# Cosine attention and a gated feed-forward on one core: the third tiles of batches 2 and 4 join pairs that run across two batches

## Chip, cores and metric

One core of a Trainium2 chip. The metric is the device time of one execution in microseconds (us). Three executions of the kernel before gave 402.96, 403.22 and 403.63 us; the median is 403.22 us.

## What is computed

The reference, cut to what matters: attention with normalised queries and keys, then a feed-forward layer with a clipped gate, then the output product.

```python
q_n = q / (norm(q) + 1e-06); k_n = k / (norm(k) + 1e-06)      # q, k, v: 8 x 12 x 448 x 64
attn = softmax(q_n @ k_n.T / tau)
x = (attn @ v).transpose(0, 2, 1, 3).reshape(3584, 768)
h = x @ w_in                                                   # 768 x 2048
g = h * clip(h + 3, 0, 6) / 6
out = g @ w_out                                                # 2048 x 768
```

The change lies in the last line, the **second product** `g @ w_out`.

## The kernel before

**Stages.** Twelve heads of a batch are worked on two at a time, so a batch has six turns and the kernel 48, numbered 0 to 47. A table of operations (`PLAN`) orders the first 18 turns, a loop over `i` the turns 18 to 47, and a table (`LAST`) what comes after them. While turn `i` does attention for its two heads of batch `i // 6`, TensorE also works off *units* of the feed-forward layer of an earlier batch, taken from `units[i]` in the order that is written there. Nothing is scheduled by itself: each engine works its own instructions in the order in which the code issues them.

**A turn of the loop, on TensorE.** Six score products (line 442) into the six PSUM banks of a ring, the remaining value products of the turn before (line 482), one unit, the seventh score product, the other units, and the first value products of this turn. A unit takes the next bank of the ring and may start only when the last reader of that bank is done.

**Units.** An `F` (`mm1_unit`, line 587) is one of the 16 column blocks of `x @ w_in` of a batch: six matmuls of 128x448, then a relu on ScalarE (line 596) and a product on VectorE (line 602) that writes the block's rows of `g` into the buffer `gT` (two buffers, for even and odd batches). The second product works on tiles of 128 tokens. A batch of 448 tokens has three and a half of them: an even batch keeps three whole tiles (0 to 2), and its last 64 tokens are copied (`g_left`) into the next batch's buffer, where they form tile 3 of the odd batch. Two tiles make a *pair*.

**Seven products for a pair.** With the tiles as rows and the two halves of the 2048 columns as columns, a pair is a 2x2 block matrix. `product_unit` multiplies it by the 2x2 blocks of `w_out` with seven block products instead of eight, named 1 to 7, of eight matmuls of 128x384 each (line 788). The names in the code are `product.pair`: 5.4 is product 5 of pair 4. VectorE makes five sums of blocks of `g` for a pair (`g_sum`, line 766): 7, 6 and 1 into buffers of their own (`gs`), 5 and 2 in place in `gT`. Products 2, 5 and 6 run on into the bank of 4, 3 and 1 after that bank has been read, or, written `2a` and `5a`, into a bank of their own, and are then added on GpSimd (line 829). ScalarE copies 3 and 4 into the buffers `d` and `e` (line 836) and 5 and 2 into output tiles (line 807, or 825 for `2a` and `5a`). GpSimd then makes `e = d + e`, `d = e - 5` and `e = e - 2` (lines 817, 818, 821). VectorE adds product 1 to `d` in place (line 845; product 6 waits for that, since it uses the bank of 1) and writes 6 + `e` and 7 + `d` out (line 813). There are two buffers `d`, used in turn by the pairs, and one `e`.

**Lone tiles.** Of an even batch tiles 0 and 1 are a pair, and tile 2 is left alone. `single_unit` (line 868) multiplies it by two units of 16 matmuls of 128x384, `s2.0` and `s2.1` for batch 2, after one sum (`e`) on VectorE, and VectorE copies each result out (line 878).

**What sets the order.** `TURNS` lists the products of each turn; the code mixes them with that turn's `F` units: two or three `F` and one or two products, the last of them at the turn's end. `side` lists the sums that VectorE makes at the start of a turn, before the turn's units. GpSimd works per turn: in odd turns first two copies of keys (`km`, line 399), then a square (line 236), a normalisation (line 293), a cast of values (line 312), and at the end what the pairs ask for. The queue of SyncE carries loads, stores and the two transposing transfers that bring normalised keys and queries (`tT`, line 350) and attention results (`xT`, lines 528 and 540) into place, all in program order.

Of the kernel before, what the change touches and what calls it, by code (L numbers as in the profile page):

```python
# [59 lines left out]
]  # L60

LAST = [
# [3 lines left out]
]  # L66
H_BY, M1_BY = "vvvvvvpp", "pppvpppp"

# [2 lines left out]
def kernel(  # L71
# [11 lines left out]
    B, H, S, D = q.shape  # L83
# [4 lines left out]
    NP = B * HP  # L88
# [576 lines left out]


    LEFT, RIGHT = slice(0, MH), slice(MH, 2 * MH)
    PAIRS = [p for b in range(0, B, 2) for p in (((b, 0), (b, 1)), ((b + 1, 3), (b + 1, 0)), ((b + 1, 1), (b + 1, 2)))][1:]
    LOOP = 8
    summed, g_summed, issued_products = set(), set(), set()  # L670
    banks, parts, ready = {}, {}, set()
    late_sums = [
# [36 lines left out]
    def sum_of(n, what):  # L709

        if what == "e":
            return gs["1"] if n < B - 2 else late_sums[1]["e"]
        if n < LOOP or n == len(PAIRS) - 1:
            return gs[what + str(n % 2) if what == "7" else what]
        return late_sums[n % 2][what]

    def d_and_e(n):
        if n < LOOP:
# [29 lines left out]
    def g_sum(n, what):  # L748

        if what == "e":  # L750
            t = 2 + n % 2
            o, x, y, op = sum_of(n, "e"), half(n, t, 0), half(n, t, 1), ALU.add
        else:
            a11, a12, a21, a22 = (block(n, i, k) for i in range(2) for k in range(2))
# [11 lines left out]
        nc.vector.tensor_tensor(out=o[:, :, :], in0=x, in1=y, op=op)  # L766
        g_summed.add((n, what))

    def product_unit(n, name, end=None, apart=False):

        need = {"3": ["y3"], "4": ["y4"], "1": "1", "6": "6", "7": "7"}.get(name, [])
        assert all((x, c) in summed for x in need for c in range(KC))
        if name not in "34":
            assert (n, name) in g_summed
        base = None if apart else {"2": "4", "5": "3", "6": "1"}.get(name)
        if base is None:
            banks[n, name] = bank_of(None, 1)
        ps, key = banks.pop((n, base)) if base else banks[n, name]
        c0, width = (MH // 2 * end, MH // 2) if end in (0, 1) else (0, MH)
        if name in "167":  # L780
            lhs, rhs = sum_of(n, name), w_sum[name]
        else:
            i, k = {"3": (0, 0), "4": (1, 1), "2": (1, 0), "5": (0, 1)}[name]
            m = LEFT if name in "42" else RIGHT
            lhs, rhs = block(n, i, k), w_out_sb[:, :, m].rearrange("p (c k) m -> p c k m", k=2)[:, :, k, :]
        m = ps[:, c0 : c0 + width]
        for c in range(KC):
            nc.tensor.matmul(  # L788
                m,
                lhs[:, c, :],  # L790
                rhs[:, c, c0 : c0 + width],
                start=(base is None and c == 0),
                stop=(c == KC - 1),
                skip_group_check=True,
            )
        issued_products.add((n, name))
        d, e = d_and_e(n)
        if base is None and name in "34":
            unread[key] = 1 + ((n, name) not in APART)

        def done(i, o, cols):
            unread[key] = 0
            result(*PAIRS[n][i], cols, o, end)

        def copied(i, cols):
            o = out_tile()
            nc.scalar.copy(out=o[:, :], in_=m)
            parts[n, name] = o
            done(i, o, cols)

        def added(i, cols, x):
            parts[n, name] = o = out_tile()
            nc.vector.tensor_tensor(out=o[:, 0:width], in0=m, in1=x[:, c0 : c0 + width], op=ALU.add)
            done(i, o, slice(cols.start + c0, cols.start + c0 + width))

        def both():
            nc.gpsimd.tensor_tensor(out=e, in0=d, in1=e, op=ALU.add)
            nc.gpsimd.tensor_tensor(out=d, in0=e, in1=parts[n, "5"][:, :], op=ALU.subtract)

        def rest():  # L820
            nc.gpsimd.tensor_tensor(out=e, in0=e, in1=parts[n, "2"][:, :], op=ALU.subtract)

        def added_later(i, cols, x):
            parts[n, name] = o = out_tile()
            nc.scalar.copy(out=o[:, :], in_=m)
            unread[key] = 0

            def add():
                nc.gpsimd.tensor_tensor(out=o[:, :], in0=o[:, :], in1=x, op=ALU.add)
                result(*PAIRS[n][i], cols, o)  # L830

            post["p"].append(add)

        def finish():
            if name in "34":
                nc.scalar.copy(out={"3": d, "4": e}[name], in_=m)
                unread[key] -= 1
            elif apart:
                added_later(*{"5": (0, RIGHT, d), "2": (1, LEFT, e)}[name])
            elif name == "5":  # L840
                copied(0, RIGHT)
            elif name == "2":
                copied(1, LEFT)
            elif name == "1":
                nc.vector.tensor_tensor(out=d, in0=m, in1=d, op=ALU.add)
# [214 lines left out]
    def products(text):  # L1060
# [10 lines left out]

    TURNS = {
# [5 lines left out]
    }  # L1078
    APART = {(n, y) for n in range(len(PAIRS)) for x, y in (("5a", "3"), ("2a", "4")) if f"{x}.{n}" in " ".join(TURNS.values()).split()}
    side = {  # L1080
        18: [(weight_sums, "y4", KC // 2, KC // 2)], 19: sums(0, "62"), 20: sums(0, "1"),
        21: sums(1, "75"), 22: sums(1, "621"),
        25: sums(2, "75"), 26: sums(2, "62"), 27: sums(2, "1"), 28: [(g_left, 2)], 29: sums(2, "e"),
        31: sums(3, "75"), 32: sums(3, "62"), 33: sums(3, "1"),
        34: sums(4, "75"), 35: sums(4, "621"), 37: [(g_left, 4)],
        38: sums(5, "75"), 39: sums(5, "62"), 40: sums(5, "1"), 41: sums(4, "e"),
        43: sums(6, "75"), 44: sums(6, "62"), 45: sums(6, "1"), 46: sums(7, "75"), 47: sums(7, "62"),
    }
    w_sums = [(w_sum_of, x, p) for p in range(FCN // 4) for x in "15672"]
    late = {44: "p", 45: "ppppp", 46: "pp"}  # L1090
# [2 lines left out]
    for b in range(2, B - 1):  # L1093
        first = firsts(b, *range(FCN))
        for n, x in enumerate([0, 3, 3, 3, 3, 2]):
            i = (b + 1) * HP + n
            u = carry + [first.pop(0) for _ in range(x)]
            carry = []
            *p, last = products(TURNS[i])
# [7 lines left out]

    assert len(carry) == 2
    units[NP] = [x for line in LAST for x in listed(line)]
    units[NP] += products("3.9 4.9") + sums(9, "1") + products("5.9") + sums(10, "75") + products("2.9 3.10") + sums(10, "62")  # L1110
    units[NP] += products("4.10 5.10") + sums(10, "1") + products("2.10 1.9 1.10")
    units[NP] += [(product_unit, n, x, 2) for n, x in ((9, "7"), (9, "6"), (10, "6"))]
    units[NP] += [(product_unit, 10, "7", x) for x in range(2)]

    FG = d_ff // 4
    weights = [
# [198 lines left out]
```

## Time and profile before

| | |
|---|---|
| median of 3 executions | 403.22 us |
| profiled execution, its own time | 403.54 us |
| its span, first to last instruction | 401.7 us |
| outside the span (403.54 - 401.7) | 1.8 us |
| mean granted TensorE clock | 0.998 |
| TensorE matmul busy | 392.0 us, 98% |
| VectorE, ScalarE, GpSimd busy | 300.9, 280.2, 262.8 us |

How to read it: a group row gives line, engine, operation, the tiles written and read, the shape and a count, then busy time and the mean length of one in ns. A row of the timeline gives the start and length of an instruction, or of a run of like ones (x8), and in brackets how long its engine had been idle before it and for whom it waited. Matmuls overlap, so a run of eight ends later than the next one starts; the distance between starts is what a unit costs.

### The profile page before, as it was taken

The numbers are of one execution on the slowest core, as the hardware profiler recorded it, in microseconds if no ns is written. First come the engines' busy times: TensorE is split into PE (matmuls) and PEld (weight loads), VectorE is DVE, ScalarE is ACT, GpSimd is POOL, SyncE is SP. The second block draws the span as 40 slices with busy tenths as digits, with TensorE's granted clock in tenths as the row PEclk, the third lists the DMA queues.
The fourth block names the chain that finished last, engine by engine and source line by source line (L and its number), as shares of the span: only waits on it lengthen the run. The fifth ranks groups of instructions, "written<-read, shape, count | busy, mean of one in ns | idle before, by whom it ended". The sixth has DMA issues, their size and how long they took to land.

```text
span 401.7 us, 9814 instructions
## 1 busy us (share of the span) xinstructions
PE 392.0 (98%) x3743; PEld 239.4 (60%) x3743; DVE 300.9 (75%) x535; ACT 280.2 (70%) x615; POOL 262.8 (65%) x253
## 2 busy tenths in 40 slices
PE   7988999999999999999999999999999999999996
PEld 5656556555665556655555556556555556687563
DVE  7998787877588777777857887587656676888863
ACT  5999989887377687787768768768758755265330
POOL 6899936753644996598486875776674893344270
PEclk9999999999999999999999999999999999999999
DMA  8999999698868658686779748966763522130133
GB/s 288 317 237 227 200 226 250 137 202 191 194 156 200 146 115 223 172 214 137 182 192 203 166 117 164 180 187 140 187 154 80 111 47 55 34 79 21 39 81 97
DMA packets 93166, 63.75 MB, mean 159 GB/s; under 512 B 56128, under 2 KB 93120, under 8 KB 93120
## 3 DMA queue, kind: packets, MB, share of 16 engines
q1 hardware_dynamic: 87408, 56.45, 59.6%
q0 software_dynamic: 5312, 6.29, 9.6%
q8 instruction: 29, 0.48, 0.5%
q10 hardware_dynamic: 400, 0.39, 0.3%
q14 instruction: 17, 0.14, 0.1%
HBM read 45.61 MB, written 11.01 MB: 141 GB/s over the span
## 4 chain that ended last, share of the span: by engine, by line
PE 91%; ACT 4%; DVE 4%; issue 1%; ACTq 0%; DVEq 0%
PE M L587 21%; PE M L788 16%; PE PV L482 11%; PE Z L587 6%; PE M L442 6%; PE Y L587 5%; PE Z L788 5%; PE Y L788 5%; PE M L868 4%; PE M L634 3%; ACT at L460 2%; PE PV L1136 2%; PE M L947 2%; PE Y L442 1%; PE Z L442 1%; DVE n L248 1%
## 5 line engine op out<-in xcount | busy, mean ns | idle before, releaser
L460 ACT ACTIVATE at<-M 128x448 bf16<-128x448 f32 x194 | 96.6, 562 | 23.2 <-PE M L442 20.6
L587 PE MATMUL M<-xT,w_in_sb 128*128 128x448 bf16 x462 | 99.2, 352 | 0.2
L587 PEld LDWEIGHTS <-w_in_sb 128*128 128x128 bf16 x696 | 65.3, 98 | 56.8 <-issue 2.8
L293 POOL TENSOR_TENSOR nrm<-big,r 128x896 bf16<-128x896 f32 (+1 forms) x47 | 78.7, 1679 | 15.4 <-issue 5.5
L236 POOL TENSOR_TENSOR big<-big 128x896 f32<-128x896 f32 (+5 forms) x45 | 68.5, 1528 | 12.9 <-DVE gT L602 8.3
L482 PEld LDWEIGHTS <-at 128*128 128x128 bf16 (+1 forms) x1536 | 54.1, 97 | 19.9 <-issue 12.1
L602 DVE SCALAR_TENSOR_TENSOR gT<-u,M 128x448 bf16<-128x448 bf16 x73 | 44.6, 618 | 28.5 <-ACT u L596 27.8
L482 PE MATMUL PV<-vx,at 128*128 128x65 bf16 (+1 forms) x1536 | 62.7, 193 | 0.0
L596 ACT ACTIVATE u<-M,bias 128x448 bf16<-128x448 f32 x77 | 50.2, 656 | 15.1 <-PE M L587 14.7
L399 POOL COPY km<-tT 64x128 bf16<-64x128 bf16 x34 | 14.4, 423 | 60.8 <-DMA tT<-nrm 26.3
L248 DVE TENSOR_REDUCE n<-big 128x14 f32<-128x896 f32 (+1 forms) x50 | 51.6, 1038 | 0.3 <-ACT big L234 0.2
L788 PEld LDWEIGHTS <-gT 128*128 128x128 bf16 x288 | 27.8, 98 | 19.0 <-DVE gT L766 0.2
L788 PE MATMUL M<-w_out_sb,gT 128*128 128x384 bf16 x192 | 35.0, 326 | 0.0
L503 DVE TENSOR_TENSOR on<-PV,rc 128x512 bf16<-128x512 f32 x48 | 33.2, 692 | 1.7
L442 PE MATMUL M<-tT,kz 64*128 64x448 bf16 (+1 forms) x171 | 30.9, 351 | 0.5 <-ACT at L460 0.5
L460 ACT ACTIVATE at<-Y 128x448 bf16<-128x448 f32 x50 | 28.1, 562 | 4.3 <-PE Z L442 4.3
L788 PEld LDWEIGHTS <-gs 128*128 128x128 bf16 x224 | 21.5, 98 | 14.7 <-DVE gs L766 0.4
L312 POOL CAST vx<-big 128x512 bf16<-128x512 f32 x39 | 28.3, 730 | 2.9 <-DMA big<-in_v_dram 2.8
L460 ACT ACTIVATE at<-Z 128x448 bf16<-128x448 f32 x50 | 28.1, 563 | 2.6 <-PE M L442 2.6
L587 PE MATMUL Z<-xT,w_in_sb 128*128 128x448 bf16 x120 | 26.0, 353 | 0.0
L587 PE MATMUL Y<-xT,w_in_sb 128*128 128x448 bf16 x114 | 24.7, 352 | 0.0
L766 DVE TENSOR_TENSOR gs<-gT 128x1024 bf16<-128x1024 bf16 x26 | 23.5, 904 | 0.0
(165 smaller groups left out, 641.4 us busy)
## 6 DMA issues: line engine op xcount, KB each, us to landing
big<-in_k_dram SPq DMA_DIRECT2D x24, 448.0 KB, 4.9
big<-in_q_dram SPq DMA_DIRECT2D x24, 448.0 KB, 4.3
out_dram<-o SPq DMA_DIRECT2D x107, 96.0 KB, 2.2
big<-in_v_dram SPq DMA_DIRECT2D x48, 128.0 KB, 4.6
big<-in_v_dram SPq DMA_DIRECT2D x48, 96.0 KB, 4.5
w_in_sb<-in_moe_w_in_dram POOLq DMA_DIRECT2D x8, 384.0 KB, 9.1
w_out_sb<-in_moe_w_out_dram POOLq DMA_DIRECT2D x4, 768.0 KB, 10.6
tT<-nrm SPq DMA_TRANSPOSE x34, 2.8
```

Source lines behind the costliest of these rows:

```text
L236: engines[e].tensor_tensor(out=o, in0=i, in1=i, op=ALU.mult)
L248: nc.vector.tensor_reduce(out=n2_and_r[0][:, d % 2, j % 2, c], in_=sq[:, :, :, :].rearrange("p g c d -> p (g c) d")[:, c, :], axis=AX.X, o ...
L293: engines[e].tensor_tensor(out=nrm[:, :, g, :].rearrange("p c g d -> p g c d"), in0=raw_of[j][:, g, :, :], in1=n2_and_r[4][:, d % 2, j % 2, :]
L312: (engines[e].copy if e == "a" else engines[e].tensor_copy)(out=o, in_=f)
L442: nc.tensor.matmul(o, ks, qt[rows], start=True, stop=True)
L460: nc.scalar.activation(out=o, in_=x, func=AF.Exp, scale=inv_tau)
L482: nc.tensor.matmul(pv_out(j, h), at[rows, n, q_cols(i // HP, j)], vt[rows, 3 + h if name == "M" else 5 * h + int(name[1]), :], start=(name ...
L503: nc.vector.tensor_tensor(out=on[:, :, :, :].rearrange("p j h d -> p h j d"), in0=pv4[:, :, :, 0:D], in1=rc[:, :, :].to_broadcast([128, 2, ...
L587: nc.tensor.matmul(ps[:, 0:S], w_in_sb[:, cc, fc * 128 : (fc + 1) * 128], x[:, cc, 0:S], start=(cc == 0), stop=(cc == CC - 1),)
L596: nc.scalar.activation(out=u[:, :], in_=ps[:, 0:S], func=AF.Relu, bias=half_bias, scale=1.0 / 6.0)
L602: nc.vector.scalar_tensor_tensor(out=g[:, fc, c0 : c0 + S], in0=u[:, :], scalar=1.0, in1=ps[:, 0:S], op0=ALU.min, op1=ALU.mult,)
L788: nc.tensor.matmul(m, lhs[:, c, :], rhs[:, c, c0 : c0 + width], start=(base is None and c == 0), stop=(c == KC - 1), skip_group_check=True,)
```

## The change

`PAIRS` is now cut from one list of tiles that runs through batches 1 to 7, without tile 2 of batch 6. So tile 2 of batch 2 is paired with tile 3 of batch 3 (pair 3), and tile 2 of batch 3 with tile 0 of batch 4 (pair 5); the lone tiles of batches 2 and 4 are gone, and the pairs after them are numbered one higher. There are 12 pairs instead of 11. In a pair across batches (`ACROSS`) the second tile is ready later than the first: sum 5 is made before sum 7 and goes into the buffer of sum 6 instead of in place. `TURNS` and `side` are written anew for turns 25 to 42; an `f` in `TURNS` now places an `F` by hand. Turns 43 to 47 and `LAST` keep their order, with the new pair numbers.

```diff
-    PAIRS = [p for b in range(0, B, 2) for p in (((b, 0), (b, 1)), ((b + 1, 3), (b + 1, 0)), ((b + 1, 1), (b + 1, 2)))][1:]
-    LOOP = 8
+    TILES = [(b, t) for b in range(1, B) for t in ((3, 0, 1, 2) if b % 2 else (0, 1, 2))]
+    TILES.remove((B - 2, 2))
+    PAIRS = list(zip(TILES[0::2], TILES[1::2]))
+    ACROSS = [n for n, (x, y) in enumerate(PAIRS) if x[0] + 1 == y[0]]
+    LOOP = 9
...
-            for w in {"2": "6", "5": "7"}.get(what, ""):
+            for w in {"2": "6", "5": "" if n in ACROSS else "7"}.get(what, ""):
...
+            if what == "5" and n in ACROSS:
+                o = gs["6"]
...
-            lhs, rhs = block(n, i, k), w_out_sb[:, :, m].rearrange("p (c k) m -> p c k m", k=2)[:, :, k, :]
+            lhs = gs["6"] if name == "5" and n in ACROSS else block(n, i, k)
+            rhs = w_out_sb[:, :, m].rearrange("p (c k) m -> p c k m", k=2)[:, :, k, :]
...
     TURNS = {
-        24: "7.0 7.1", 25: "3.2 5a.2", 26: "4.2 2.2", 27: "1.2 6.2", 28: "7.2", 29: "s2.0", 30: "s2.1",
-        31: "3.3 5a.3", 32: "4.3 2.3", 33: "1.3 6.3", 34: "3.4 5.4", 35: "4.4 2.4", 36: "1.4 6.4",
-        37: "7.3 7.4", 38: "3.5 5.5", 39: "4.5 2.5", 40: "1.5 6.5", 41: "s4.0", 42: "7.5 s4.1",
-        43: "3.6 5a.6", 44: "4.6 2.6", 45: "1.6 6.6", 46: "3.7 5.7", 47: "7.6",
+        24: "7.0 7.1", 25: "3.2", 26: "5a.2", 27: "4.2 2.2", 28: "1.2 6.2", 29: "3.3 5.3", 30: "7.2",
+        31: "4.3 2a.3", 32: "1.3 6.3", 33: "3.4 5.4", 34: "4.4 2.4", 35: "1.4 6.4", 36: "7.3 3.5 5.5",
+        37: "f f 4.5 f 7.4", 38: "2a.5", 39: "f 1.5 f 6.5 f 7.5", 40: "3.6 5.6", 41: "4.6 2.6", 42: "1.6 f 6.6 f 7.6",
+        43: "3.7 5a.7", 44: "4.7 2.7", 45: "1.7 6.7", 46: "3.8 5.8", 47: "7.7",
...
     side = {
-        31: sums(3, "75"), 32: sums(3, "62"), 33: sums(3, "1"),
+        31: sums(3, "7612"), 33: sums(4, "75"), 34: sums(4, "621"), 36: sums(5, "5"),
```

Two places of the new order matter below. The first is VectorE in turn 42, from the reciprocal (line 502) that follows the value products of turn 41. Before:

```order
L502 RECIPROCAL rc<-PV 128x8
L503 TENSOR_TENSOR on<-PV,rc 128x2x4x64
L602 SCALAR_TENSOR_TENSOR gT_72<-u,M_694 128x448
L813 TENSOR_TENSOR o<-Y,big 128x384
L602 SCALAR_TENSOR_TENSOR gT_72<-u,Z 128x448
L878 COPY o<-M_696 128x384
```

And in the changed kernel, where lines after 668 have other numbers (line 852 is the addition of product 1 to `d` that was line 845, line 820 the sum that was line 813):

```order
L502 RECIPROCAL rc<-PV 128x8
L503 TENSOR_TENSOR on<-PV,rc 128x2x4x64
L852 TENSOR_TENSOR big<-M_695,big 128x384
L602 SCALAR_TENSOR_TENSOR gT_72<-u,Z 128x448
L820 TENSOR_TENSOR o<-M_695,big 128x384
L602 SCALAR_TENSOR_TENSOR gT_72<-u,M_696 128x448
L820 TENSOR_TENSOR o<-M_697,big 128x384
```

What moved: product 1 of pair 6 is now the first unit of the turn, so its addition to `d` stands at the head of VectorE's queue there, right behind the end of turn 41, in which products 4 and 2 of that pair are made.

The second place is VectorE in turn 31. Before:

```order
L503 TENSOR_TENSOR on<-PV,rc 128x2x4x64
L766 TENSOR_TENSOR gs_79<-gT_72 128x1024
L766 TENSOR_TENSOR gT_72<-gT_72 128x8x128
L602 SCALAR_TENSOR_TENSOR gT_71<-u,Y 128x448
L389 COPY kz_80<-tT_83 128x384
```

And in the changed kernel (line 772 is the sum that was line 766):

```order
L503 TENSOR_TENSOR on<-PV,rc 128x2x4x64
L772 TENSOR_TENSOR gs_79<-gT_71,gT_72 128x1024
L772 TENSOR_TENSOR gs_77<-gT_72,gT_71 128x1024
L772 TENSOR_TENSOR gs_76<-gT_71,gT_72 128x1024
L772 TENSOR_TENSOR gT_72<-gT_72 128x8x128
L602 SCALAR_TENSOR_TENSOR gT_71<-u,M_695 128x448
L389 COPY kz_80<-tT_83 128x384
```

What moved: four sums stand in one turn instead of two, and the last of them, in place in `gT`, is what product 2a.3 at the end of this same turn reads.

More of the change, by code (lines that the diff above doesn't have):

```diff
@@ L714, in sum_of @@
             return gs[what + str(n % 2) if what == "7" else what]
-        return late_sums[n % 2][what]
+        return late_sums[(n - LOOP) % 2][what]
     def d_and_e(n):
@@ L753, in g_sum @@
         else:
-            a11, a12, a21, a22 = (block(n, i, k) for i in range(2) for k in range(2))
-            for w in {"2": "6", "5": "7"}.get(what, ""):
+            a11, a12 = (block(n, 0, k) for k in range(2))
+            a21, a22 = (block(n, 1, k) for k in range(2)) if what != "5" else (a11, a12)
+            for w in {"2": "6", "5": "" if n in ACROSS else "7"}.get(what, ""):
                 assert (n, w) in g_summed
@@ L1082 @@
         21: sums(1, "75"), 22: sums(1, "621"),
-        25: sums(2, "75"), 26: sums(2, "62"), 27: sums(2, "1"), 28: [(g_left, 2)], 29: sums(2, "e"),
-        31: sums(3, "75"), 32: sums(3, "62"), 33: sums(3, "1"),
-        34: sums(4, "75"), 35: sums(4, "621"), 37: [(g_left, 4)],
-        38: sums(5, "75"), 39: sums(5, "62"), 40: sums(5, "1"), 41: sums(4, "e"),
-        43: sums(6, "75"), 44: sums(6, "62"), 45: sums(6, "1"), 46: sums(7, "75"), 47: sums(7, "62"),
+        25: sums(2, "75"), 27: sums(2, "621"), 28: [(g_left, 2)], 29: sums(3, "5"),
+        31: sums(3, "7612"), 33: sums(4, "75"), 34: sums(4, "621"), 36: sums(5, "5"),
+        37: sums(5, "761"), 38: sums(5, "2"), 39: [(g_left, 4)],
+        40: sums(6, "75"), 41: sums(6, "621"),
+        43: sums(7, "75"), 44: sums(7, "62"), 45: sums(7, "1"), 46: sums(8, "75"), 47: sums(8, "62"),
     }
@@ L1098 @@
             carry = []
+            if "f" in TURNS[i]:
+                units[i] = [x for y in TURNS[i].split() for x in ([u.pop(0)] if y == "f" else products(y))]
+                assert not u
+                continue
             *p, last = products(TURNS[i])
@@ L1109 @@
     units[NP] = [x for line in LAST for x in listed(line)]
[L1110 to L1113, printed above, removed]
+    units[NP] += products("3.10 4.10") + sums(10, "1") + products("5.10") + sums(11, "75") + products("2.10 3.11") + sums(11, "62")
+    units[NP] += products("4.11 5.11") + sums(11, "1") + products("2.11 1.10 1.11")
+    units[NP] += [(product_unit, n, x, 2) for n, x in ((10, "7"), (10, "6"), (11, "6"))]
+    units[NP] += [(product_unit, 11, "7", x) for x in range(2)]
     FG = d_ff // 4
```

6 rows, old and new, of the table LAST are left out of this document.

## The prediction

> **What bounds the kernel now.** I read the head of the page first: is one engine full from end to end? These are the engine's share and its 40 slices.
>
> ```profile
> PE 392.0 (98%) x3743; PEld 239.4 (60%) x3743; DVE 300.9 (75%) x535; ACT 280.2 (70%) x615; POOL 262.8 (65%) x253
> ...
> PE   7988999999999999999999999999999999999996
> ```
>
> TensorE is full from the third slice on. Since matmuls overlap, a full slice could still hide waits. So next I read the busy times in the stretch that the change touches (turns 25 to 42 lie in it): PE, weight loads, VectorE, ScalarE, GpSimd, then granted clock and DMA.
>
> ```profile
> 150.00:338.00 188.00, 188.00 (x1786) 110.62 (x1785) 135.98 (x222) 137.98 (x311) 133.96 (x121) 1.00 0.68 155
> ```
>
> TensorE has no gap in 188 us, at full clock, and the list of its waits has no entry there. The other three have 50 us of idle time each, a good quarter. So a matmul that goes is time gained, one for one; a matmul that has to wait is time lost; work on the others costs nothing as long as TensorE does not wait for it.
>
> **Term 1: TensorE's work.** The lone tile of batch 2 in turn 29, and what follows it:
>
> ```profile
> 201.24 1.46 PE L868 MATMUL M<-w_out_sb,gs 128*128 128x384 bf16 x8
> 202.54 1.46 PE L868 MATMUL M<-w_out_sb,gT 128*128 128x384 bf16 x8
> 203.84 0.54 PE L482 MATMUL PV<-vx,at 128*128 128x65 bf16 x10
> ```
>
> From start to start eight matmuls take 202.54 - 201.24 = 1.30 us, 0.1625 us each. Two lone tiles are four units of 16, 64 matmuls. One more pair is seven products of 8, 56 matmuls of the same shape. The change takes out 8 matmuls: **-1.30 us**. By turns: 25, 26, 30 and 38 each have one product (1.30 us) less, 28, 36 and 39 one more, and the rest as many as before, a single unit counted as two. From turn 43 on the order is as before.
>
> The Trainium skill (TensorE: Matmul & The Clock Gate, section Back-to-back issue gap) gives two spacings: a sustained one of about 81 ns for 128 columns and 131 ns for 512, and an isolated one of N/2.4 + 2.5 ns. The first would make 384 columns about 114 ns, as an estimate between the two, and the eight matmuls 0.9 us; the trace has 162.5 ns and agrees with the second, so the measurement decides.
>
> **Term 2: work beside it.**
>
> ```profile
> L766 DVE TENSOR_TENSOR gs<-gT 128x1024 bf16<-128x1024 bf16 x26 | 23.5, 904 | 0.0
> ...
> L813 DVE TENSOR_TENSOR o<-M,big 128x384 f32<-128x384 f32 x12 | 6.7, 556 | 1.6 <-PE M L788 0.7 <-issue 0.3
> ...
> L878 DVE COPY o<-M 128x384 f32<-128x384 f32 x6 | 3.3, 554 | 3.8 <-PE M L868 3.8
> ```
>
> VectorE: five sums come, two sums `e` go, three additions come and four copies go: 3 x 0.90 + 3 x 0.56 - 4 x 0.55 = 2.2 us more. ScalarE gets four copies and GpSimd three sums and one `2a` addition, of about 0.5 and 1 us each. The idle 50 us of each cover this in total. Without the cover it would be 2 to 4 us; it is at the places below that cover could fail. I cost the rest at nothing. The new sums over two tensors have the shape of the `gs` row. The stores are eight DMAs out and eight in. Sum 5 of a pair across shares its buffer with sum 6, but product 5 stands a turn ahead of that sum.
>
> **Term 3: a new wait in turn 42.** Product 1.6 is now the first unit there. VectorE adds it to `d`, and for that GpSimd must have finished `d`, which it does only after turn 41. Product 6.6 waits for the addition. Before, the same order of sums and products as the new turn 41 (F, 4, F, 2, with sums 6, 2, 1) stands in turn 35, so I read its end and turn 36: GpSimd, VectorE, TensorE.
>
> ```profile
> 245.26 0.99 POOL L399 COPY km<-tT 64x128 bf16<-64x128 bf16 x2 [6.35 <-DMA tT<-nrm]
> 246.33 2.00 POOL L236 TENSOR_TENSOR big<-big 128x896 f32<-128x896 f32 x1
> 248.29 1.69 POOL L293 TENSOR_TENSOR nrm<-big,r 128x896 bf16<-128x896 f32 x1
> 249.92 0.61 POOL L312 CAST vx<-big 128x512 bf16<-128x512 f32 x1
> 250.49 0.99 POOL L817 TENSOR_TENSOR big<-big 128x384 f32<-128x384 f32 x1
> 251.56 1.00 POOL L818 TENSOR_TENSOR big<-big,o 128x384 f32<-128x384 f32 x1
> ```
> ```profile
> 252.69 0.62 DVE L602 SCALAR_TENSOR_TENSOR gT<-u,M 128x448 bf16<-128x448 bf16 x1 [1.36 <-ACT u L596]
> 253.23 0.55 DVE L845 TENSOR_TENSOR big<-Z,big 128x384 f32<-128x384 f32 x1
> ```
> ```profile
> 250.19 1.30 PE L587 MATMUL M<-xT,w_in_sb 128*128 128x448 bf16 x6
> ...
> 251.51 1.46 PE L788 MATMUL Z<-w_sum,gs 128*128 128x384 bf16 x8
> 252.81 1.30 PE L587 MATMUL M<-xT,w_in_sb 128*128 128x448 bf16 x6
> 253.95 1.30 PE L788 MATMUL Z<-w_sum,gs 128*128 128x384 bf16 x7
> ```
>
> GpSimd works without a pause from 245.26 and has `d` ready at 251.56 + 1.00 = 252.56. In turn 36 nothing waits for it: product 1 was the second unit there, its addition began at 253.23, and 6 was due at 253.95. Put 1 first, as turn 42 now does. It starts at 250.19. The seventh score (0.19) and an F (1.13) follow, so product 6 is due at 250.19 + 1.30 + 0.19 + 1.13 = 252.81. The addition can start at 252.60, 0.04 behind GpSimd, and ends 0.56 later, at 253.16. How fast TensorE then starts is seen where it did wait, for a copy on ScalarE:
>
> ```profile
> 369.55 0.35 ACT L1003 COPY gT<-Z 128x224 f32<-128x224 f32 x1
> ```
> ```profile
> 369.96 0.45 PE L947 MATMUL Z<-at,big 128*128 128x224 bf16 x3 [0.16 <-ACT gT L1003]
> ```
>
> About 0.05 us after the copy's end. So 6.6 starts at 253.21 instead of 252.81: **+0.40 us**. The bounds: 0, if GpSimd is 0.4 us earlier; 1.0, if one more GpSimd operation gets ahead. Behind the waiting addition VectorE has an F product whose relu comes later anyway, so nobody else waits.
>
> **Term 4: four sums in turn 31, and a short turn 30.** A sum that meets GpSimd at work is held:
>
> ```profile
> 177.00 1.68 POOL L236 TENSOR_TENSOR big<-big 128x896 f32<-128x896 f32 x1 [0.26 <-DVE rc L502]
> 178.64 2.14 POOL L293 TENSOR_TENSOR nrm<-big,r 128x896 bf16<-128x896 f32 x1
> ```
> ```profile
> 177.62 1.61 DVE L766 TENSOR_TENSOR gs<-gT 128x1024 bf16<-128x1024 bf16 x1
> 179.26 2.06 DVE L766 TENSOR_TENSOR gT<-gT 128x1024 bf16<-128x1024 bf16 x1
> ```
>
> The first sum ends 0.55 us after the square ends (178.68), the normalisation 1.55 us after that sum, the next sum 0.54 us after the normalisation: they take turns. In turn 31, before:
>
> ```profile
> 213.21 0.68 DVE L766 TENSOR_TENSOR gs<-gT 128x1024 bf16<-128x1024 bf16 x1
> 213.93 0.78 DVE L766 TENSOR_TENSOR gT<-gT 128x1024 bf16<-128x1024 bf16 x1
> ```
> ```profile
> 213.88 0.99 POOL L399 COPY km<-tT 64x128 bf16<-64x128 bf16 x2 [4.26 <-PE M L442]
> 214.95 1.68 POOL L236 TENSOR_TENSOR big<-big 128x896 f32<-128x896 f32 x1
> ```
> ```profile
> 213.65 1.30 PE L587 MATMUL Y<-xT,w_in_sb 128*128 128x448 bf16 x6
> 214.78 1.30 PE L587 MATMUL Z<-xT,w_in_sb 128*128 128x448 bf16 x6
> 215.92 1.30 PE L587 MATMUL M<-xT,w_in_sb 128*128 128x448 bf16 x6
> 217.05 1.46 PE L788 MATMUL M<-w_out_sb,gT 128*128 128x384 bf16 x8
> ```
>
> Four sums at a spacing of 0.72 start at 213.21, 213.93, 214.65 and 215.37. The fourth would meet the square of 214.95 and be held to about 217.5, after 217.05, when 2a.3 is due: 0.5 us. But the key copies will come later, because turn 30 gets shorter while the queue of SyncE, which brings those keys, does not:
>
> ```profile
> 209.49 1.23 SPq L528 DMA_TRANSPOSE xT<-on  x1
> 210.82 2.59 SPq L350 DMA_TRANSPOSE tT<-nrm  x2
> ```
> ```profile
> DMA to landing us min/median/max: 2.8/2.8/2.8
> ```
>
> The last line is that of the first of the two transfers of 210.82. It lands at 213.6 on the scale of turn 30, which is 213.6 + 1.30 = 214.9 on the scale of turn 31. Then the copies start at 214.9 instead of 213.88, the square comes behind them, after 215.9, and the fourth sum is done by about 216.2: no wait. I take **0**, with 0 and 0.6 as bounds. The attention results of the transfer of 209.49 must be there for the sixth matmul of the first F, 213.65 + 0.95 - 1.30 = 213.3 on the same scale; this one and its like:
>
> ```profile
> DMA to landing us min/median/max: 3.1/3.1/3.1
> ```
> ```profile
> DMA to landing us min/median/max: 2.4/3.7/4.5
> ```
>
> This transfer took 3.1 us (212.6), the median 3.7 (213.2), the longest 4.5 (214.0). So 0, at most 0.7.
>
> **The sum.** -1.30 + 0.40 + 0 = -0.90 us: 402.64 us for the profiled execution of 403.54. That execution lies 0.32 us above the median of 403.22; against the median the forecast is 402.3.
>
> **The rivals.** *No wait at all* (1.5 in 10): GpSimd reaches `d` earlier in turn 41, since its key copies in turn 35 had waited 6.35 us for a DMA. Against it: the square behind them was itself held by the third sum (2.00 us instead of 1.68), so earlier keys would not have brought it forward. It gives -1.30, 401.9 us.
>
> *Small waits in turns 30 to 32* (2.3 in 10): the transposed transfers land late or the fourth sum is held by the square, 0.5 to 0.7 us more; the margin of 0.1 us at the median landing speaks for it, the 3.1 us of this very transfer against. It gives -0.3, 402.9 us.
>
> *The sums fall into step with GpSimd* (1 in 10): if the square of turn 31 starts before the third sum, not after, the third sum ends 0.55 us behind the square (216.63 + 0.55 = 217.18), the normalisation 1.55 us later (218.73), the fourth sum at 219.27. Product 2a.3, due at 217.05, starts 2.3 us late with its weight load: -0.90 + 2.3 = +1.4, 404.6 us, slower than before. It decides at 0.3 us: the third sum is due at 214.65, the square was at 214.95. The later keys speak against it. The Trainium skill (SBUF — State Buffer, section Terms, shared port pair) says that VectorE and GpSimd hold a pair of ports for a whole instruction and that the loser fully blocks; the trace agrees (2.06 us for a sum that alone takes 0.68), and by that rule each added sum can cost a whole GpSimd instruction.
>
> **How the numbers follow.** The forecast has 5.2 in 10, the rivals 1.5, 2.3 and 1. A measurement of this kernel can tell about 0.2%, 0.81 us, from no change. The forecast lies just beyond that with its -0.90; with a spread of 0.3 us around it I put 3.2 of its 5.2 to faster and 2.0 to same. Faster: 3.2 + 1.5 = 4.7; same: 2.0 + 2.3 = 4.3; slower: 1.0. The range goes from -1.30 less 0.2 us of scatter (401.7) to the second rival with its largest wait and that scatter, -0.90 + 0.7 + 0.3 (403.3); it leaves out the third.
>
> **What would show it.** Right: TensorE has 8 matmuls fewer; its starts in turn 42 show a gap of about 0.4 us ahead of product 6.6, with the addition of line 852 starting right behind line 825; no gap ahead of 2a.3, with the keys copied about 1 us later in turn 31. Wrong: a gap in turn 31, a fourth sum of over 1.5 us, waits on the transfers in turns 25, 31 or 37, or a gap ahead of 6.5 in turn 39, where the addition to `d` also has little room.

## The result, and the profile after

The changed kernel takes 402.24 us (median of 13 executions, 401.72 to 403.24), the kernel before 403.42 us in the same series (13 executions, 402.71 to 405.89): 1.18 us less. The ratio of the two is 0.9963, 95% interval 0.9946 to 0.998. So it is faster, by 0.2 to 0.5%. Line numbers of the changed kernel are those of the section on the change (795 is the product that was 788, 772 the sum, 852 the addition of product 1 to `d`, 824 and 825 GpSimd's two operations on `e` and `d`).

The head of its page, and the stretch of turns 25 to 42 in the view by windows (PE, weight loads, VectorE, ScalarE, GpSimd, granted clock, DMA):

```profile
PE 390.0 (98%) x3735; PEld 238.3 (60%) x3735; DVE 296.1 (74%) x537; ACT 281.6 (70%) x619; POOL 266.8 (67%) x257
```
```profile
150.00:338.00 188.00, 187.91 (x1811) 110.89 (x1809) 132.60 (x226) 139.34 (x315) 137.49 (x124) 1.00 0.71 155
```

Eight matmuls fewer (3743 to 3735), and TensorE is still full. But the span fell from 401.7 to 399.8 us, by 1.9 us, more than eight matmuls can give. One must see where. A good marker is the first value product (line 482) of a turn's own heads, which TensorE works at the very end of that turn. The ends of turns 24 and 43, before and changed:

```profile
167.11 0.63 PE L482 MATMUL PV<-vx,at 128*128 128x65 bf16 x16
...
309.12 0.57 PE L482 MATMUL PV<-vx,at 128*128 128x65 bf16 x11
```
```profile
166.23 0.63 PE L482 MATMUL PV<-vx,at 128*128 128x65 bf16 x16
...
307.16 0.41 PE L482 MATMUL PV<-vx,at 128*128 128x65 bf16 x8
```

The same marker for other turns:

| end of turn | before | changed | difference |
|---|---|---|---|
| 1 | 23.49 | 22.87 | -0.62 |
| 19 | 129.94 | 129.30 | -0.64 |
| 20 | 138.01 | 137.13 | -0.88 |
| 24 | 167.11 | 166.23 | -0.88 |
| 26 | 182.76 | 179.28 | -3.48 |
| 28 | 197.15 | 194.93 | -2.22 |
| 30 | 210.53 | 207.05 | -3.48 |
| 36 | 255.25 | 253.10 | -2.15 |
| 38 | 270.93 | 267.45 | -3.48 |
| 39 | 278.76 | 276.57 | -2.19 |
| 41 | 293.31 | 291.09 | -2.22 |
| 42 | 301.30 | 299.34 | -1.96 |
| 43 | 309.12 | 307.16 | -1.96 |

Almost half of the 1.96 us is there before the first changed turn: 0.62 in the start-up and 0.24 in turn 20. In the changed turns the steps stand where they were forecast, about 1.3 us down in turns 25, 26, 30 and 38 and up in 28, 36 and 39. They leave -1.34 at the end of turn 41, and turn 42 gives 0.26 back. From the end of turn 24 to that of turn 43 (**the stretch**, below) it is 309.12 - 167.11 = 142.01 us before and 307.16 - 166.23 = 140.93 us now: the change is worth **-1.08 us**.

**Turn 42** in the changed kernel, on GpSimd (from turn 41 on), VectorE and TensorE:

```profile
287.63 1.02 POOL L399 COPY km<-tT 64x128 bf16<-64x128 bf16 x2 [6.30 <-PE M L442]
288.73 2.00 POOL L236 TENSOR_TENSOR big<-big 128x896 f32<-128x896 f32 x1
...
292.89 0.99 POOL L824 TENSOR_TENSOR big<-big 128x384 f32<-128x384 f32 x1
293.96 1.00 POOL L825 TENSOR_TENSOR big<-big,o 128x384 f32<-128x384 f32 x1
```
```profile
294.99 0.56 DVE L852 TENSOR_TENSOR big<-M,big 128x384 f32<-128x384 f32 x1 [1.14 <-POOL big L825]
```
```profile
292.73 1.46 PE L795 MATMUL M<-w_sum,gs 128*128 128x384 bf16 x8
294.02 0.35 PE L442 MATMUL Y<-tT,km 128*128 128x448 bf16 x1
294.21 1.30 PE L587 MATMUL Z<-xT,w_in_sb 128*128 128x448 bf16 x6
295.61 0.65 PE L795 MATMUL M<-w_sum,gs 128*128 128x384 bf16 x3
```

The addition of 1.6 starts 0.03 us behind line 825 (294.96), ends at 295.55, and 6.6 starts 0.06 later. From the F's start to the next unit it takes 1.40 us, where an F alone takes 1.13 to 1.14: a gap of **0.26 us**. The list of waits has no entry for it, because the modelled end of the F (295.51) covers most of it. Only the starts show it.

**Turn 31**, on VectorE, GpSimd and TensorE:

```profile
209.73 1.89 DVE L772 TENSOR_TENSOR gs<-gT,gT 128x1024 bf16<-128x1024 bf16 x3
211.53 0.78 DVE L772 TENSOR_TENSOR gT<-gT 128x1024 bf16<-128x1024 bf16 x1
```
```profile
211.11 1.36 POOL L399 COPY km<-tT 64x128 bf16<-64x128 bf16 x2 [3.99 <-PE M L587]
212.55 1.68 POOL L236 TENSOR_TENSOR big<-big 128x896 f32<-128x896 f32 x1
```
```profile
212.44 1.30 PE L587 MATMUL Z<-xT,w_in_sb 128*128 128x448 bf16 x6
213.57 1.46 PE L795 MATMUL M<-w_out_sb,gT 128*128 128x384 bf16 x8
```

The fourth sum is done at 212.31, the square starts after it, and 2a.3 follows its F at the usual 1.13 us: no wait. The copies of keys start when their transfer has landed, at 210.99; the F that the row names as their releaser reads no keys.

### The profile page after: what moved, and what is told of

Its sections match the earlier page's. It is cut to its first block, busy times and chain, and to the rows that moved or that the text cites. A ratio compares the mean times of both kernels' runs of the same rounds, so it can differ in the third digit from the quotient of the medians.

```text
span 399.8 us, 9819 instructions
## 1 busy us (share of the span) xinstructions
PE 390.0 (98%) x3735; PEld 238.3 (60%) x3735; DVE 296.1 (74%) x537; ACT 281.6 (70%) x619; POOL 266.8 (67%) x257
## 4 chain that ended last, share of the span: by engine, by line
PE 84%; ACT 5%; DMA 3%; DVE 3%; SPq 2%; POOL 2%; issue 1%; ACTq 0%; DVEq 0%; POOLq 0%
PE M L587 20%; PE M L795 17%; PE PV L482 10%; PE Z L587 6%; PE M L442 5%; PE Y L587 5%; PE Y L795 5%; PE Z L795 4%; PE M L634 3%; ACT at L460 3%; DMA big<-in_q_dram 2%; PE M L954 2%; PE Y L442 1%; PE Z L442 1%; SPq L219 1%
## 5 line engine op out<-in xcount | busy, mean ns | idle before, releaser
L460 ACT ACTIVATE at<-M 128x448 bf16<-128x448 f32 x196 | 98.1, 564 | 19.4 <-PE M L442 16.6
L587 PE MATMUL M<-xT,w_in_sb 128*128 128x448 bf16 x450 | 96.7, 352 | 0.2
L602 DVE SCALAR_TENSOR_TENSOR gT<-u,M 128x448 bf16<-128x448 bf16 x71 | 43.2, 618 | 30.7 <-ACT u L596 30.0
L596 ACT ACTIVATE u<-M,bias 128x448 bf16<-128x448 f32 x75 | 49.0, 657 | 12.4 <-PE M L587 11.4
L795 PEld LDWEIGHTS <-gT 128*128 128x128 bf16 x304 | 29.5, 98 | 20.2
L795 PE MATMUL M<-w_out_sb,gT 128*128 128x384 bf16 x200 | 36.4, 326 | 0.0
L795 PEld LDWEIGHTS <-gs 128*128 128x128 bf16 x264 | 25.5, 98 | 17.5 <-issue 0.3
L795 PE MATMUL M<-w_sum,gs 128*128 128x384 bf16 (+1 forms) x184 | 32.0, 319 | 0.1
L587 PE MATMUL Z<-xT,w_in_sb 128*128 128x448 bf16 x138 | 29.9, 353 | 0.0
L587 PE MATMUL Y<-xT,w_in_sb 128*128 128x448 bf16 x108 | 23.4, 352 | 0.0
```

What stands on the lines that cost most here:

```text
L460: nc.scalar.activation(out=o, in_=x, func=AF.Exp, scale=inv_tau)
L587: nc.tensor.matmul(ps[:, 0:S], w_in_sb[:, cc, fc * 128 : (fc + 1) * 128], x[:, cc, 0:S], start=(cc == 0), stop=(cc == CC - 1),)
L596: nc.scalar.activation(out=u[:, :], in_=ps[:, 0:S], func=AF.Relu, bias=half_bias, scale=1.0 / 6.0)
L602: nc.vector.scalar_tensor_tensor(out=g[:, fc, c0 : c0 + S], in0=u[:, :], scalar=1.0, in1=ps[:, 0:S], op0=ALU.min, op1=ALU.mult,)
L795: nc.tensor.matmul(m, lhs[:, c, :], rhs[:, c, c0 : c0 + width], start=(base is None and c == 0), stop=(c == KC - 1), skip_group_check=True,)
```

## The experiments

Theory: -1.30 us from the matmuls, plus a wait in turn 42 that GpSimd's chain sets; the rest of the 1.96 us is not the change. The rival is that the gain sits in the start-up and in turn 20, which the change would have shortened. (The expectations call that place turn 19, and there "from the first value product of turn 42" means the one at turn 42's start.) All edits are to the changed kernel. The times of one series were taken on one chip, with the kernel before beside them: 403.47 us for the first four rows, 403.49 for the next four, 403.32 for the last three.

| run | median us | ratio to before, 95% | end of turn 1 | the stretch | against 140.93 |
|---|---|---|---|---|---|
| again | 402.24 | 0.9967 (0.9942 to 0.9992) | 25.08 | 140.92 | -0.01 |
| no_wait | 402.49 | 0.9965 (0.9943 to 0.9987) | 23.02 | 140.68 | -0.25 |
| long_wait | 402.98 | 0.9984 (0.9961 to 1.0007) | 23.31 | 141.72 | +0.79 |
| eight_more | 403.67 | 0.9994 (0.9971 to 1.0017) | 22.80 | 142.23 | +1.30 |
| before_again | one, 405.72 | | 25.91 | 142.02 | +1.09 |
| two_sums | 404.67 | 1.0033 (1.0006 to 1.006) | 25.14 | 142.56 | +1.63 |
| long_30 | 404.46 | 1.0025 (0.9997 to 1.0053) | 25.14 | 142.24 | +1.31 |
| thin | 398.34 | 0.9874 (0.9857 to 0.9892) | 23.55 | 137.06 | -3.87 |
| sums_40 | 401.89 | 0.9964 (0.9952 to 0.9976) | 22.91 | 140.71 | -0.22 |
| twice_e | 404.38 | 1.0026 (1.0005 to 1.0048) | 23.66 | 143.27 | +2.34 |
| best | 401.68 | 0.9957 (0.9945 to 0.997) | 23.43 | 140.69 | -0.24 |

### Both kernels a second time: again and before_again

No edit.

> The changed kernel as it is, for a second profile and more times. Theory: in the first profiles it reached turn 43 1.96 us earlier than the kernel before, of which -1.30 us are the 8 matmuls, +0.26 us a wait ahead of product 6.6 in turn 42, and the remaining -0.9 us (0.63 in turns 0 and 1, 0.25 in turn 19) differences between executions that the change has nothing to do with. So here: turn 42 again with a wait of 0.2 to 0.3 us, the start of turn 2 anywhere within 0.7 us of the two seen so far (26.65 and 26.02 us), and a median 1.0 to 1.2 us below that of the kernel before. Rival (the change itself makes the start and turn 19 shorter): turn 2 starts at 26.0 us again, turn 19 has no wait again, and the median is about 1.9 us below.

> The kernel before as it is, for a second profile of its start and of turn 19. Theory (start-up and turn 19 differ from execution to execution, the same for both kernels): the start of turn 2 and the waits in turn 19 need not repeat (26.65 us and 0.24 us in the first profile). Rival (they belong to the kernel): both repeat within 0.1 us.

The ends of turns 24 and 43, in the changed kernel again and in the kernel before again:

```profile
168.96 0.60 PE L482 MATMUL PV<-vx,at 128*128 128x65 bf16 x14
...
309.88 0.41 PE L482 MATMUL PV<-vx,at 128*128 128x65 bf16 x8
```
```profile
169.27 0.60 PE L482 MATMUL PV<-vx,at 128*128 128x65 bf16 x14
...
311.29 0.57 PE L482 MATMUL PV<-vx,at 128*128 128x65 bf16 x12
```

The stretch repeats within 0.01 us in each: 140.92 and 142.02. The start does not. Turn 1 ended at 25.08 and 25.91 us, 2.2 and 2.4 us later than in the first profiles of the same two kernels, so that this profile of the changed kernel has a longer span (402.5) than the first one of the kernel before (401.7). The scatter is larger than the 0.7 us I expected. Turn 20 lost 0.24 us again, but now in the changed kernel (8.06 us from marker to marker, where 7.82 or 7.83 is usual; turn 19 lost 0.3 us there too) and not in the kernel before (7.82). So neither belongs to the change; the rival falls.

### Price of the matmuls: eight_more

```diff
-        for c in range(KC):
+        for c in [*range(KC)] * (1 + ((n, name) == (4, "3"))):
             nc.tensor.matmul(
```

> The changed kernel with the eight matmuls of product 3.4 in turn 33 done twice (the second time writes the same over the first), so that TensorE has as many matmuls as in the kernel before. Theory: TensorE is full, so eight matmuls cost 8 x 0.1625 = 1.30 us: 403.5 us, as long as before or 0.1 longer, and turn 33 takes 1.30 us more. Rival (the matmuls were partly covered and the gain came from the start-up and from turn 19): under 0.7 us more, 402.9 us or less.

The stretch grew by 1.30 us and the median by 1.43, to that of the kernel before within what these times can tell (ratio 0.9994). The time comes in turn 33, which ends at 231.78 instead of 230.56 while turn 32 ends at 222.62 instead of 222.70: 9.16 us for 7.86. Eight matmuls cost their full 1.30 us.

### The wait in turn 42: no_wait, long_wait, twice_e, sums_40

Product 6.6 one F later (no_wait); one more GpSimd operation ahead of line 824 (long_wait); two more behind it (twice_e); one sum less in turn 41 (sums_40):

```diff
-42: "1.6 f 6.6 f 7.6",
+42: "1.6 f f 6.6 7.6",
```
```diff
         def both():
+            if n == 6:
+                nc.gpsimd.tensor_tensor(out=wide_late[0], in0=d, in1=d, op=ALU.add)
             nc.gpsimd.tensor_tensor(out=e, in0=d, in1=e, op=ALU.add)
```
```diff
             nc.gpsimd.tensor_tensor(out=e, in0=d, in1=e, op=ALU.add)
+            if n == 6:
+                nc.gpsimd.tensor_tensor(out=e, in0=e, in1=d, op=ALU.subtract)
+                nc.gpsimd.tensor_tensor(out=e, in0=e, in1=d, op=ALU.add)
```
```diff
-        40: sums(6, "75"), 41: sums(6, "621"),
+        40: sums(6, "756"), 41: sums(6, "21"),
```

> The changed kernel with the units of turn 42 in the order 1.6, F, F, 6.6, 7.6, so that product 6.6 comes one F (1.13 us) later. Theory (6.6 waits for the addition of 1.6 to d, and that for GpSimd's subtraction of line 825): the addition still starts right behind line 825, but 6.6 is now due 0.87 us after it could start, so TensorE has no gap in turn 42, and turn 43 starts 0.26 us earlier after turn 42 than in the changed kernel (from first value product of turn 42 to that of turn 43: 8.25 us there, 8.0 here). Time 402.0 us, which the times alone cannot tell from 402.24. Rival (the gap belongs to the place, not to d: the bank, or the weights): a gap of about 0.26 us stays, ahead of whatever stands second.

> The changed kernel with one more GpSimd operation (d + d into a buffer that is not used until later, 128x384, about 1.0 us) ahead of line 824 of pair 6 at the end of turn 41. Theory: d comes 1.0 to 1.1 us later, so the gap ahead of 6.6 grows from 0.26 to 1.2 to 1.4 us, and the time by as much: 403.2 to 403.4 us. Rival (the gap is not for d): it stays at 0.26 us, since GpSimd is idle for a third of the time, and the time at 402.2.

> The changed kernel with two more GpSimd operations behind line 824 of pair 6 (e less d, e plus d again, so that e is the same but for rounding), each about 1.07 us from start to start. Theory: d comes 2.1 us later, and the gap ahead of 6.6 grows from 0.26 to 2.4 us, one for one, as the one operation of 0.82 us in the run before made it 1.04; the time 404.4 us. Rival (a longer wait lets GpSimd or VectorE catch up elsewhere, or uses up the slack of turn 43): the time grows by clearly less or more than the gap.

> The changed kernel with sum 6 of pair 6 made at the start of turn 40 instead of turn 41, so that two sums stand in turn 41 (2 and 1) and three in turn 40. In the changed kernel the third sum of turn 41 overlaps GpSimd's square, which then takes 2.00 instead of 1.68 us, and the two copies of keys take 1.02 instead of 0.66. Theory (GpSimd's unbroken chain copies, square, normalisation, cast, line 824, line 825 sets when d is ready, so whatever stretches it makes the wait): the square takes 1.68 us, d is ready at least 0.3 us earlier against the turn, the gap ahead of 6.6 falls from 0.26 us to nothing. Rival (the chain is set by its start, when the keys land, and the sums do not matter): the gap stays at 0.2 us or more.

In long_wait the extra result went over a buffer that at this point still held loaded input, so a part of the output is computed from wrong data; the amount of work is the same.

In no_wait the addition on VectorE still waits for line 825, but TensorE goes from F to F and from the second F to 6.6 in 1.13 to 1.14 us each:

```profile
295.31 0.56 DVE L852 TENSOR_TENSOR big<-M,big 128x384 f32<-128x384 f32 x1 [1.14 <-POOL big L825]
```
```profile
294.53 1.30 PE L587 MATMUL Z<-xT,w_in_sb 128*128 128x448 bf16 x6
295.67 1.30 PE L587 MATMUL M<-xT,w_in_sb 128*128 128x448 bf16 x6
296.80 2.76 PE L795 MATMUL M<-w_sum,gs 128*128 128x384 bf16 x16
```

The gap is gone and the stretch 0.25 us shorter; the median, 402.49, does not resolve that, as expected. The gap is not bound to the place. In long_wait the extra operation (line 825 of that kernel, which pushes the others down by two) took 0.82 us, not the 1.0 I had given it, and the gap grew by nearly that:

```profile
293.31 0.82 POOL L825 TENSOR_TENSOR big<-big 128x384 f32<-128x384 f32 x1
```
```profile
294.63 1.30 PE L587 MATMUL Z<-xT,w_in_sb 128*128 128x448 bf16 x6
296.80 0.97 PE L795 MATMUL M<-w_sum,gs 128*128 128x384 bf16 x5 [0.88 <-DVE big L854]
```

296.80 - 294.63 = 2.17, less 1.13: 1.04 us, 0.78 more. With the two operations of twice_e it is 2.40 us, 2.14 more, all of it in the stretch. So 6.6 follows `d` one for one. The stretch of twice_e has another 0.19 us, which belongs to turn 37 (below).

In sums_40 two sums stand in turn 41. GpSimd's square then takes 1.68 us instead of 2.00:

```profile
288.75 1.68 POOL L236 TENSOR_TENSOR big<-big 128x896 f32<-128x896 f32 x1
290.51 1.69 POOL L293 TENSOR_TENSOR nrm<-big,r 128x896 bf16<-128x896 f32 x1
...
293.79 1.00 POOL L825 TENSOR_TENSOR big<-big,o 128x384 f32<-128x384 f32 x1
```
```profile
294.26 1.30 PE L587 MATMUL Z<-xT,w_in_sb 128*128 128x448 bf16 x6
295.43 0.81 PE L795 MATMUL M<-w_sum,gs 128*128 128x384 bf16 x4
```

`d` is ready at 294.79, 0.22 us earlier against the turn (turn 41 ended at 291.14 here, 291.09 in the changed kernel), and the gap falls to 0.04 us. I expected 0.3 and no gap; 0.08 us pass between the square's end (290.43) and the normalisation's start, which in the changed kernel overlap by 0.04. So most of the wait came from the third sum of turn 41, which the square met. On VectorE in the changed kernel:

```profile
287.08 0.68 DVE L772 TENSOR_TENSOR gs<-gT 128x1024 bf16<-128x1024 bf16 x1
287.80 0.69 DVE L772 TENSOR_TENSOR gT<-gT 128x1024 bf16<-128x1024 bf16 x1
288.41 0.78 DVE L772 TENSOR_TENSOR gs<-gT 128x1024 bf16<-128x1024 bf16 x1
```

The third ends at 289.19, and the square, which had started at 288.73, ends 1.54 us behind that, at 290.73. This is the spacing of 1.55 us that the prediction read off a normalisation in its term 4.

### The edge in turn 31: two_sums and long_30

Two more sums ahead of sum 2 in turn 31 (two_sums); product 7.2 done twice in turn 30 (long_30):

```diff
-        31: sums(3, "7612"),
+        31: sums(3, "761772"),
```
```diff
-        for c in range(KC):
+        for c in [*range(KC)] * (1 + ((n, name) == (2, "7"))):
```

> The changed kernel with sum 7 of pair 3 made three times instead of once in turn 31, ahead of sum 2, so six sums stand where there were four. In the changed kernel the four start at 209.73 us and every 0.60 us behind it, the last at 211.53, and GpSimd's square starts at 212.55, after it. Theory (a sum that meets GpSimd at work ends 0.55 us behind GpSimd's operation): sum 2 would start at 212.73, behind the start of the square, and end at 214.8 to 215.1, so product 2a.3, due at 213.57, waits 1.2 to 1.6 us: 403.4 to 403.8 us. Rival (sums cost only their own time): sum 2 ends at 213.5, and 2a.3 waits 0.1 us at most; 402.3 us. Third possibility: VectorE's later products with the relu hold up banks, and TensorE waits in turn 32 too, more than 1.6 us in all.

> The changed kernel with the eight matmuls of product 7.2 at the end of turn 30 done twice, so that turn 30 takes 1.30 us more, as long as before. Theory of the prediction (four sums in turn 31 found room because the keys come about 1 us later against turn 31, since TensorE's turn 30 got shorter and the queue of SyncE did not): here the keys come earlier against turn 31, the square starts before the fourth sum or during it, that sum takes 1.5 to 2.0 us instead of 0.78, and product 2a.3 waits 0 to 0.5 us; time 402.24 + 1.30 + 0 to 0.5 = 403.5 to 404.0 us. Rival (the keys are copied when TensorE's seventh score product is done, whenever they came): copies and square keep their place against the turn, the fourth sum takes 0.78 us again, and the time is 403.5 us.

In two_sums the last sum starts 0.41 us after GpSimd's square (214.81), is held until 0.55 us after the square's end, and TensorE waits for it:

```profile
214.81 2.03 POOL L236 TENSOR_TENSOR big<-big 128x896 f32<-128x896 f32 x1
```
```profile
215.22 2.17 DVE L772 TENSOR_TENSOR gT<-gT 128x1024 bf16<-128x1024 bf16 x1
```
```profile
214.71 1.30 PE L587 MATMUL Z<-xT,w_in_sb 128*128 128x448 bf16 x6
217.44 1.31 PE L795 MATMUL M<-w_out_sb,gT 128*128 128x384 bf16 x7 [1.44 <-DVE gT L772]
```

217.44 - 214.71 - 1.13 = 1.60 us, the upper end of what I expected, and the stretch is 1.63 longer. No wait followed in turn 32. (The medians of two_sums and long_30 rose by more than the stretch, 2.43 and 2.22 us. Both profiled executions started late, and with that their own times add up: 401.72 + 1.63 + 25.14 - 22.87 = 405.62 for 405.63 us measured in two_sums, and 405.30 for 405.29 in long_30. Whether the other executions of these two kernels started late as well was not recorded.)

In long_30 turn 30 is as long as before the change, and turn 31 is where the two ideas part:

```profile
213.98 1.46 POOL L399 COPY km<-tT 64x128 bf16<-64x128 bf16 x2 [4.58 <-PE M L442]
215.52 2.00 POOL L236 TENSOR_TENSOR big<-big 128x896 f32<-128x896 f32 x1
```
```profile
213.31 1.98 DVE L772 TENSOR_TENSOR gs<-gT,gT 128x1024 bf16<-128x1024 bf16 x3
215.21 0.78 DVE L772 TENSOR_TENSOR gT<-gT 128x1024 bf16<-128x1024 bf16 x1
```
```profile
217.15 1.46 PE L795 MATMUL M<-w_out_sb,gT 128*128 128x384 bf16 x8
```

The keys' copies do come earlier against 2a.3: 217.15 - 213.98 = 3.17 us ahead of it, as before the change (217.05 - 213.88 = 3.17), against 213.57 - 211.11 = 2.46 in the changed kernel. But the fourth sum still takes 0.78 us, since it starts 0.31 us ahead of the square, and the stretch grows by the matmuls alone (+1.31). My expectation was half right: the keys move, the sum is not held. Here and before the change the copies wait for the seventh score product, in the changed kernel for the transfer; so the rival, by which they keep their place, is wrong too, though its time for the sum is right.

### How far the cover reaches: thin

```diff
+        last = KC - 1 - (2 <= n <= 6)
-        for c in range(KC):
+        for c in range(last + 1):
```

> The changed kernel with the last of the eight matmuls left out of each product of pairs 2 to 6 (35 products in turns 25 to 42; the last eighth of their sums is not computed). Theory (TensorE alone sets the time there): 35 x 0.1625 = 5.69 us less, 396.6 us, with no gap on TensorE but that of turn 42. Rival (the other engines have a quarter of idle time, but their chains within a turn do not): turns become 0.3 us shorter per product, waits for keys, for sums and for d come up, and the gain is 3 to 5 us, 397.5 to 399 us.

The stretch lost 3.87 us of the 5.69 that 35 matmuls are worth, and the median 3.9: the rival is right. The largest wait is again that for `d` in turn 42 (the list of waits in turns 25 to 42, and the head of the chain of waits that ends in it; line numbers of this kernel are one higher from 796 on):

```profile
PE M L796 <- DVE big L853: 1.2, 1, 1.2
```
```profile
280.45 4.71 DMA tT<-nrm
...
285.29 0.46 POOL km L399
...
285.80 0.30 POOL km L399
...
286.17 1.68 POOL big L236
```

By the starts it is 1.37 us instead of 0.26, so its growth makes up 1.11 of the 1.82 us that are missing; the rest are losses of at most 0.16 us each, which were not followed up. That chain now starts with the keys' transfer (4.71 us to land), no longer with TensorE's own work, and does not get shorter when TensorE's turns do. The idle quarter of each engine let the change's 1.30 us through but for 0.26; of 5.69 us it let only 3.87 through.

### Both waits away: best

```diff
-42: "1.6 f 6.6 f 7.6",
+42: "1.6 f f 6.6 7.6",
...
-        18: [(weight_sums, "y4", KC // 2, KC // 2)], 19: sums(0, "62"), 20: sums(0, "1"),
+        18: [(weight_sums, "y4", KC // 2, KC // 2)], 19: sums(0, "621"),
```

> The changed kernel with both places at which TensorE was seen to wait taken away: turn 42 in the order 1.6, F, F, 6.6, 7.6, and sum 1 of pair 0 made in turn 19 rather than at the start of turn 20, where in some executions it met GpSimd at work and TensorE waited 0.1 to 0.25 us. Theory: no gap in turns 19 to 47, from the end of turn 24 to the end of turn 43 140.66 us instead of 140.92, and a median about 0.3 us below that of the changed kernel, 401.9 us; the times alone cannot tell 0.3 us. Rival (sum 1 in turn 19 meets GpSimd there instead): a gap in turn 19 or 20 stays.

No gap from turn 19 to 47, the stretch 140.69 us, 1.32 less than before. The median 401.68 and the ratio 0.9957 are the lowest of the runs that do all the work (thin leaves some out), but the interval holds the changed kernel's 0.9963 too: that `best` beats it is shown by the stretch, not by the times. Turn 20 took its usual 7.82 us, as it does in most runs anyway, so that part of the edit is not shown to help.

## Why the prediction was right, step by step

The forecast was -0.90 us against the profiled execution; the stretch gives -1.08, the medians -1.18. That the median, 402.24, lies so close to the 402.32 that 403.22 - 0.90 gives is partly luck: the median of the kernel before rose by 0.20 us with ten more executions, and the difference came out 0.28 us larger than forecast. (One row was misread, without effect on the sum: slices three and four of TensorE show 8, so it is full from the fifth on, not the third.)

**Term 1, the matmuls, right.** -1.34 us by the markers at the end of turn 41, in the turns that were named, and +1.30 when eight are put back. The isolated spacing of the Trainium skill's formula (TensorE: Matmul & The Clock Gate, Back-to-back issue gap), 162.5 ns at 384 columns, holds for this; its sustained figures would have made eight_more cost about 0.9 us, an estimate from that page, and it cost 1.30.

**Term 2, the work beside, right here, and only just.** No new wait came from it in the changed turns. VectorE's busy time in the window did not even rise by the 2.2 us worked out; it fell from 135.98 to 132.60. How long sums are held differs more than the change adds: in that window the sums alone took 33.22 us before (34 of them), and 30.30 (36) and 33.78 us (37) in the two profiles of the changed kernel. The other place that was named, product 6.5 in turn 39, had no wait: the addition ended at 272.67, and 6.5 started at 272.84, 1.14 us behind its F. But thin shows that the cover does not scale.

**Term 3, the wait in turn 42, right in its mechanism, too large in its size: 0.26 us, not 0.40.** The part that failed is the sentence against the first rival, that earlier keys would not have brought the square forward. Taken from the start of product 1, GpSimd's copies began 250.19 - 245.26 = 4.93 us ahead in turn 35 before the change, where they waited for a transfer, and 292.73 - 287.63 = 5.10 us ahead in turn 41 now, where they wait for the seventh score product. The square followed its copies by 0.08 us both times, and `d` came 252.56 - 250.19 = 2.37 us behind product 1's start there and 294.96 - 292.73 = 2.23 us here. The 0.14 us went through the chain to TensorE. It is a firm number: again, eight_more, two_sums and long_30, which leave turn 41 alone, all have a gap of 0.26 us there. The rival "no wait at all" saw this cause but gave it all of the 0.40.

**Term 4, no wait in turn 31, right, for a reason that was only partly needed.** The keys do come later, by 0.71 us against 2a.3 where about 1 was forecast. But the 0.5 us feared without that does not appear in long_30. Two things had been missed: these sums follow each other every 0.60 us and not every 0.72, and the keys' copies, meeting these sums, take 1.36 to 1.46 us instead of 0.99 and push the square back. The 0.72 was read off a pair in which the second sum writes in place over a block that the first still reads, so that it has to wait for the first; that two different tensors are read is not the reason, as turn 41 above shows (0.72 us to the sum in place, 0.61 us from it to the next, all within `gT`). In turn 31 now, sum 1 stands between sum 6 and the sum in place that has to wait for it. The margin in the changed kernel is 212.55 - 211.53 = 1.02 us. That the sums can fall into step with GpSimd, the slower rival, is real, but it needs two sums more (two_sums). The rule of the Trainium skill (SBUF — State Buffer, section Terms, shared port pair) that the loser fully blocks fits the 2.17 us of that sum; the end of the hold, 0.55 us behind the square, is from the traces.

The transfers in turns 25, 31 and 37 cost nothing in the changed kernel's profile. In turn 37 that was close: in twice_e, whose edit lies later, the transfer took 5.3 us instead of 5.1 to land (at 256.63), and the last matmul of the first F, which reads it, started 0.04 us after that, 0.19 us late (changed, then twice_e):

```profile
254.73 1.30 PE L587 MATMUL M<-xT,w_in_sb 128*128 128x448 bf16 x6
```
```profile
255.53 1.49 PE L587 MATMUL M<-xT,w_in_sb 128*128 128x448 bf16 x6
```

## What to carry to other kernels

Where one engine is full, count its instructions: a change that takes some away gains their time, less what the new order makes it wait, and a wait of some tenths shows only in the starts, not in the list of waits. Follow the chain that feeds such a wait back to what starts it, since each tenth there arrives at the end; a chain that starts with the full engine's own work moves with it, and one that starts with a transfer does not. When profiles differ by less than the start-up scatters, compare the same stretch between two markers instead of the spans.

## What the runs showed of the hardware that was not expected

- The start-up alone scatters by 3.1 us between profiled executions: turn 1 ended between 22.80 and 25.91 us, in both kernels, while the stretch of 141 us repeats within 0.01 us.
- A sum that needs nothing of the one before it starts 0.60 us behind it (1.89 us for three), 0.08 us before that one's recorded end; one in place over a block that the sum before it reads starts 0.72 us behind it, 0.04 us after that end.
- A GpSimd operation (square or normalisation) that starts while a sum runs ends 1.54 to 1.55 us behind that sum's end, whichever of the two it is and in both kernels.
- GpSimd's small copies of keys are stretched by VectorE's sums as well: 0.30 us for one in thin that meets none, 1.36 and 1.46 us for two in turn 31 (changed and long_30) beside the four sums.
